# Hash attention and a gated block on one core: parts kept back across a batch's joint, and hash evictions spread among the parts

## The chip, the cores and the metric

One core of a Trainium2 chip. Time is device time in microseconds (us) of one execution; medians of the runs are quoted. TensorE multiplies, VectorE (DVE in the profile) and ScalarE (ACT) work elementwise, and both read the products from PSUM. An **eviction** below reads a hash product out of PSUM and writes its bits: those of k on VectorE, those of q on ScalarE.

## The reference, cut to what matters

```python
# q, k, v: (4, 8, 768, 64); proj: (64, 6)
q_bucket = sum((q @ proj > 0) * powers);  k_bucket likewise        # 6-bit hashes
scores = where(q_bucket == k_bucket, q @ k.T / 8, -1e9)
attn   = softmax(scores) @ v                                       # per batch and head
x      = attn.transpose(0, 2, 1, 3).reshape(3072, 512)
g      = x @ w_gate                                                # 512 -> 1536
out    = (g * sigmoid(g) * (x @ w_val)) @ w_out                    # the gated block
```

## The kernel before

The kernel walks over 16 pairs of heads (four pairs for each of four batches), 12 units of attention to a pair. One **turn** of the main loop does two units: scores, attend, and then parts of the gated block of the *previous* batch, which fill TensorE while the other engines work. The parts stand in the list `atoms` with their sizes; in the seven-product groups below a part is one step, of size 1: two products, which the trace shows as four matmul instructions. A down part (down-projection) has size 2 and shows as six, with 512 columns each.

For batches 1 to 3 the up-projection uses seven products per group (steps 0 to 6) in place of eight. This needs sums of x and of the weights, made on VectorE when the batch's attention ends:

```python
def norm(u):                       # end of half a pair
    ps = score_tile("sum")[:, 0, :] if atoms else bank("sum")
    ...                            # sum product, reciprocal, xT
    if pr == NP - 1 and half == 1:
        push_ffn(b)                # for b > 0: eight sums of x, then sums of weights, then new atoms

def gate(t, g):                    # ScalarE, then VectorE
    nc.scalar.activation(th, g, AF.Tanh, scale=0.5)
    nc.vector.scalar_tensor_tensor(out=t, in0=th, scalar=1.0, in1=g, op0=ALU.add, op1=ALU.mult)
# group steps: 0 copies its product on ScalarE; 1 and 2 one VectorE sum each;
# 3 a gate; 4 two sums and a gate; 5 and 6 a sum and a gate.
# In the value groups a VectorE product takes the place of each gate.
```

For pairs 8 to 15 the four hash products of the next pair share one PSUM tile, taken from the two score buffers:

```python
def hash_blocks():
    ps = front_bank("hps")         # for these pairs: a score buffer
    where = [(name, half) for name in "kq" for half in range(2)]
    for i, (name, half) in enumerate(where):
        nc.tensor.matmul(ps[i * BLOCK : (i + 1) * BLOCK, 0:HQ], ...)
    for i, (name, half) in enumerate(where):
        for to in (0, D):
            sign(name, half, slice(to, to + BLOCK), ps, slice(i * BLOCK, (i + 1) * BLOCK))
            # k: VectorE, q: ScalarE; so k k k k q q q q
```

And the main loop:

```python
for u in range(0, N + 2, 2):       # one turn
    score(u); score(u + 1)
    while due: norm(due.pop(0))
    for x in left: attend(x)
    mine = [up to two steps of the next pair: transposes, hash products]
    ...
    credit += 6.2 if n < 2 * NP else 5.6
    spent = 0
    while atoms and credit >= atoms[0][0]:
        size, atom = atoms.pop(0)
        credit -= size
        spent += size
        atom()
        narrow_on(2 * size)        # conversion of weights, VectorE
        if mine and spent >= 2:
            spent = 0
            mine.pop(0)()
    for step in mine: step()
```

The softmax here doesn't subtract the row's maximum and nothing guards it: scores larger than these inputs give would overflow.

Of the kernel before, what the change touches and what calls it, by code (L numbers as in the profile page):

```python
# [17 lines left out]
def kernel(  # L18
# [13 lines left out]
    B, H, S, D = q.shape  # L32
# [5 lines left out]
    BLOCK = 32  # L38
    NP = H // 2
# [30 lines left out]
    def bank(name):  # L70
        return mm_ps.tile([P, 512], FP32, tag="mm", name=name)
# [40 lines left out]
    def load(n):  # L112
        for name in "qkv":
            fetch(n, name, nc.sync)
# [20 lines left out]
    for _ in range(9):  # L135
        ps = bank("idle")
# [96 lines left out]
    def narrow_on(n):  # L233
        for _ in range(n):
            next(narrowing, None)
# [10 lines left out]
    def front_bank(name):  # L246

        if len(T) > 2 * 2 * NP:
            return score_tile(name)[:, 0, :]
        return bank(name)  # L250

    def front(n):


        def transpose(name, half):
            if (name, n) not in T:
                T[name, n] = opnd.tile([P, S], FP32, tag=name + "T", name=name + "T")
            ps = front_bank("tps")
            for i in range(CH):
                nc.tensor.transpose(ps[:, i * P : (i + 1) * P],  # L260
                                    raws[name, n][:, half * CH + i, :, :].rearrange("p h d -> p (h d)"),
                                    ident)
            nc.scalar.copy(T[name, n][:, half * HQ : (half + 1) * HQ], ps[:, 0:HQ])

        bits["q", n] = sides["q", n % 2]
        bits["k", n] = sides["k", n % 2]

        def sign(name, half, to, ps, at):
            o = bits[name, n][to, half * HQ : (half + 1) * HQ]
            if name == "q":  # L270
                nc.scalar.activation(o, ps[at, 0:HQ], AF.Sign, bias=nudge[to])  # L271
            else:
                nc.vector.tensor_scalar(o, ps[at, 0:HQ], scalar1=above_k[to], scalar2=times_k[to],  # L273
                                        op0=ALU.is_gt, op1=ALU.mult)

        def hash_bits(name, half):
            ps = front_bank("hps")
            nc.tensor.matmul(ps[:, 0:HQ], hash_w[name], T[name, n][:, half * HQ : (half + 1) * HQ],  # L278
                             start=True, stop=True)
            sign(name, half, slice(0, P), ps, slice(0, P))  # L280

        def hash_blocks():

            ps = front_bank("hps")
            where = [(name, half) for name in "kq" for half in range(2)]
            for i, (name, half) in enumerate(where):
                nc.tensor.matmul(ps[i * BLOCK : (i + 1) * BLOCK, 0:HQ], hash_w[name][:, 0:BLOCK],  # L287
                                 T[name, n][:, half * HQ : (half + 1) * HQ], start=True, stop=True)
            for i, (name, half) in enumerate(where):
                for to in (0, D):  # L290
                    sign(name, half, slice(to, to + BLOCK), ps, slice(i * BLOCK, (i + 1) * BLOCK))

        def transpose_blocks(name):
            T[name, n] = opnd.tile([P, S], FP32, tag=name + "T", name=name + "T")
            nc.vector.transpose(T[name, n], raws[name, n].rearrange("p c h d -> p (c h d)"))

        steps = []
        if n > NP:

            for name in "qk":  # L300
                steps.append(lambda name=name: transpose_blocks(name))
        if n >= 2 * NP:
            return steps + [hash_blocks]
        order = [("q", 0), ("k", 0), ("k", 1), ("q", 1)]
        for at in (order[0:2], order[2:3], order[3:4]) if n == 0 else (order,):
            if n <= NP:
                for x in at:
                    steps.append(lambda x=x: transpose(*x))
            for x in at:
                steps.append(lambda x=x: hash_bits(*x))  # L310
        return steps
# [7 lines left out]
    def score(u):  # L319
        n, half, c = units[u]  # L320
        qs = slice(half * HQ, (half + 1) * HQ)
        ks = slice(c * P, (c + 1) * P)
        sc = score_tile("sc")
        for x, start in ((bits, True), (T, False)):
            for h in range(2):
                rows = slice(h * D, (h + 1) * D)
                nc.tensor.matmul(sc[:, h, 0:HQ], x["k", n][rows, ks], x["q", n][rows, qs],  # L327
                                 start=start, stop=not start)
        nc.scalar.activation(ring[u % RING][:, :, 0:HQ], sc[:, :, 0:HQ], AF.Exp, scale=SCALE)  # L329

    def attend(u):
        n, half, c = units[u]
        a = ring[u % RING]
        if c == 0:
            av[n, half] = av_ps.tile([P, 512], FP32, tag="av", name="av")
        ps = av[n, half]
        for h in range(2):
            nc.tensor.matmul(ps[h * D : (h + 1) * D, 0:AW], raws["v", n][:, h, c, :], a[:, h, :],  # L338
                             start=c == 0, stop=c == NCH - 1)
        if c == 1:  # L340
            acc[n, half] = att.tile([P, 2, HQ], FP32, tag="acc", name="acc", bufs=1)
            nc.vector.scalar_tensor_tensor(out=acc[n, half], in0=ring[(u - 1) % RING][:, :, 0:HQ],
                                           scalar=S * EPS / P, in1=a[:, :, 0:HQ],
                                           op0=ALU.add, op1=ALU.add)
        elif c > 1:
            nc.vector.tensor_tensor(acc[n, half], acc[n, half], a[:, :, 0:HQ], op=ALU.add)  # L346
        if c == NCH - 1:
            av[n, half] = att.tile([P, AW], FP32, tag="avs", name="avs", bufs=1)
            nc.scalar.copy(av[n, half], ps[:, 0:AW])

    def norm(u):
        n, half, _ = units[u]
        b, pr = pairs[n]
        if half == 0:
            xT[b, pr] = xp.tile([P, S], FP32, tag="xT", name="xT")
        ps = score_tile("sum")[:, 0, :] if atoms else bank("sum")
        t = acc.pop((n, half))
        for h in range(2):
            nc.tensor.matmul(ps[h * D : (h + 1) * D, 0:HQ], ones, t[:, h, :], start=True, stop=True)  # L359
        a = av.pop((n, half))  # L360
        r = att.tile([P, HQ], FP32, tag="r", name="r", bufs=1)
        nc.vector.reciprocal(r, ps[:, 0:HQ])  # L362
        e = att.tile([P, 1], FP32, tag="e", name="e")
        nc.vector.tensor_scalar(e, a[:, HQ : HQ + 1], scalar1=EPS, scalar2=None, op0=ALU.mult)
        nc.vector.scalar_tensor_tensor(out=xT[b, pr][:, half * HQ : (half + 1) * HQ],
                                       in0=a[:, 0:HQ], scalar=e, in1=r,
                                       op0=ALU.add, op1=ALU.mult)
        if pr == NP - 1 and half == 1:
            push_ffn(b)
# [181 lines left out]
    credit = 0.0  # L551
    left = []
    due = []
    for u in range(0, N + 2, 2):
        n, at = divmod(u, per)
        if u < N:
            if at == (4 if n == 0 else 0) and n + 1 < len(pairs):
                steps.extend(front(n + 1))
            if at == per - 2 and n + 2 < len(pairs):
                load(n + 2)  # L560
            score(u)
            score(u + 1)
        while due:
            norm(due.pop(0))
        for x in left:
            attend(x)
            if units[x][2] == NCH - 1:
                due.append(x)
        left = [u, u + 1]
        mine = [steps.pop(0) for _ in range(2) if (u < 4 or u % per >= 2) and steps]  # L570
        if not atoms:
            credit = 0.0
            for step in mine:
                step()
            narrow_on(3 if u % 12 == 6 else 2)
            continue

        credit += 6.2 if n < 2 * NP else 5.6
        spent = 0
        while atoms and credit >= atoms[0][0]:  # L580
            size, atom = atoms.pop(0)
            credit -= size
            spent += size
            atom()
            narrow_on(2 * size)
            if mine and spent >= 2:
                spent = 0
                mine.pop(0)()
        for step in mine:
            step()  # L590
    while due:
        norm(due.pop(0))
    for _, atom in atoms:
# [33 lines left out]
```

## Time and profile before

| | before |
|---|---|
| time, median of the 3 runs at hand | 1128.71 us |
| TensorE busy, of a span of 1128.2 us | 1093.0 us |
| TensorE idle (span less busy) | 35.2 us |
| of it, waits at three joints between batches | 15.8 us |
| of it, waits that hash evictions cause, three kinds | 6.1 us |

TensorE is the bound, so only its idle time and its clock matter. A matmul at half the granted clock counts as busy, only longer: a loss of clock shows as more "busy", a wait as idle (at a granted clock of 0.50, four matmuls that usually take 1.45 us take 2.90 in the prediction's lines).

### The profile page before, as it was taken

What the parts mean: (1) busy time and instruction counts of PE and PEld (TensorE: products, weight loads), DVE (VectorE), ACT (ScalarE), POOL (GpSimd) and SP (SyncE); (2) the same over time, 40 slices, a digit from 0 to 9 for tenths busy, and PEclk for the clock granted to TensorE, in tenths of its full rate; (3) what the DMA queues carried; (4) which work ended last, traced back from release to release, by engine and by line L of the source; (5) the groups of instructions that cost most, each with busy time, mean ns of one, the idle gap of its engine ahead of it and who ended that gap; (6) DMA issues with size and microseconds to landing.
All of it is one profiled execution on the core that took longest, in us unless ns stands there. A gap on an engine that the chain in (4) does not pass through costs nothing.

```text
span 1128.2 us, 10837 instructions
## 1 busy us (share of the span) xinstructions
PE 1093.0 (97%) x4213; PEld 525.5 (47%) x4213; DVE 700.7 (62%) x1143; ACT 284.8 (25%) x449; POOL 21.1 (2%) x57
## 2 busy tenths in 40 slices
PE   8999999999999989999999997999999997999998
PEld 3444445555544444545544443454544443555543
DVE  4899989999932267777761337667674223667400
ACT  4545222222222213222222222223231120111100
POOL 1000000000000000000000000000000000000000
PEclk9999999999999989999999998999999998999999
DMA  5333422424200220010002021001000000000000
GB/s 141 90 97 64 115 74 89 104 75 117 75 24 19 47 52 1 15 28 1 15 1 61 19 61 29 1 15 29 15 0 10 10 19 19 1 1 0 1 28 28
DMA packets 97843, 44.74 MB, mean 40 GB/s; under 512 B 86016, under 2 KB 90112, under 8 KB 97792
## 3 DMA queue, kind: packets, MB, share of 16 engines
q1 hardware_dynamic: 92032, 26.03, 10.2%
q0 software_dynamic: 4960, 17.83, 5.1%
q8 instruction: 33, 0.54, 0.2%
q10 hardware_dynamic: 800, 0.20, 0.1%
q14 instruction: 18, 0.15, 0.0%
HBM read 37.75 MB, written 6.29 MB: 39 GB/s over the span
## 4 chain that ended last, share of the span: by engine, by line
PE 89%; DVE 6%; ACT 3%; issue 1%; DMA 0%; POOL 0%; SPq 0%; ACTq 0%; DVEq 0%; POOLq 0%
PE up L450 28%; PE po L526 22%; PE sc L327 12%; PE up L396 11%; PE av L338 11%; PE sum L359 2%; ACT A L329 2%; PE hps L278 2%; DVE r L362 1%; DVE kb L273 1%; ACT qb L271 1%; DVE xc L423 1%; DVE acc L346 1%; PE tps L260 1%; PE hps L287 0%
## 5 line engine op out<-in xcount | busy, mean ns | idle before, releaser
L526 PE MATMUL po<-wo,ht 128*128 128x512 f32 x576 | 254.8, 597 | 0.0
L329 ACT ACTIVATE A<-sc 128x768 f32<-128x768 f32 x192 | 154.0, 812 | 213.4 <-PE sc L327 201.2
L362 DVE RECIPROCAL r<-sum 128x384 f32<-128x384 f32 x32 | 81.8, 2556 | 176.0 <-PE sum L359 176.0
L526 PEld LDWEIGHTS po<-wo,ht 128*128 128x128 f32 x576 | 107.3, 190 | 140.2 <-issue 139.1
L327 PE MATMUL sc<-qT,kT 64*128 64x384 f32 x768 | 155.7, 484 | 0.0
L338 PE MATMUL av<-A,vraw 128*64 128x386 f32 x768 | 144.1, 496 | 0.0
L346 DVE TENSOR_TENSOR acc<-acc,A 128x768 f32<-128x768 f32 x128 | 122.2, 954 | 29.8 <-ACT A L329 24.4
L450 PE MATMUL up<-xT,ws 128*128 128x384 f32 x288 | 108.7, 501 | 0.0
L338 PEld LDWEIGHTS av<-A,vraw 128*64 128x64 f32 x768 | 49.3, 136 | 81.4 <-issue 81.2
L327 PEld LDWEIGHTS sc<-qT,kT 64*128 64x128 f32 x768 | 69.2, 190 | 21.0 <-issue 21.0
L450 PEld LDWEIGHTS up<-xT,ws 128*128 128x128 f32 x288 | 55.2, 195 | 44.6 <-issue 7.2
L462 DVE TENSOR_TENSOR ht<-ht,up 128x384 f32<-128x384 f32 x108 | 57.0, 548 | 25.9 <-PE up L450 23.3
L450 PE MATMUL up<-xc,ws 128*128 128x384 f32 x144 | 57.3, 523 | 15.8 <-DVE ws L442 15.8
L462 DVE TENSOR_TENSOR c<-c,up 128x384 f32<-128x384 f32 x108 | 57.6, 549 | 23.7 <-PE up L450 23.0
L396 PE MATMUL up<-xT,wg 128*128 128x384 f32 x192 | 66.9, 491 | 0.4 <-DVE kb L273 0.4
L396 PE MATMUL up<-xT,wv 128*128 128x384 f32 x192 | 66.9, 491 | 0.3 <-DVE wv L226 0.3
L377 ACT ACTIVATE c<-up 128x384 f32<-128x384 f32 x42 | 20.6, 491 | 184.0 <-PE up L396 100.9
L327 PE MATMUL sc<-qb,kb 64*128 64x384 bf16 x384 | 63.9, 329 | 1.7 <-ACT qb L271 0.9
L450 PE MATMUL up<-xT,wv 128*128 128x384 f32 x144 | 54.3, 501 | 2.9 <-ACT ht L483 2.9
L450 PE MATMUL up<-xc,wg 128*128 128x384 f32 x144 | 53.9, 498 | 2.3 <-DVE c L378 2.3
L530 ACT COPY o<-po 128x512 f32<-128x512 f32 x24 | 14.1, 587 | 159.1 <-PE po L526 158.8
L450 PE MATMUL up<-xc,wv 128*128 128x384 f32 x144 | 53.2, 492 | 0.0
(99 smaller groups left out, 934.8 us busy)
## 6 DMA issues: line engine op xcount, KB each, us to landing
vraw<-in_v_dram SPq DMA_DIRECT2D x16, 384.0 KB, 3.3
words<-in_moe_w_val_dram POOLq DMA_DIRECT2D x12, 512.0 KB, 3.8
words<-in_moe_w_out_dram POOLq DMA_DIRECT2D x12, 512.0 KB, 3.6
out_dram<-o SPq DMA_DIRECT2D x24, 256.0 KB, 2.0
words<-in_moe_w_gate_dram POOLq DMA_DIRECT2D x10, 512.0 KB, 3.9
qraw<-in_q_dram SPq DMA_DIRECT2D x48, 96.0 KB, 3.4
kraw<-in_k_dram SPq DMA_DIRECT2D x46, 96.0 KB, 3.3
qraw<-in_q_dram SPq DMA_DIRECT2D x8, 192.0 KB, 3.6
```

The source lines that it names most:

```text
L278: nc.tensor.matmul(ps[:, 0:HQ], hash_w[name], T[name, n][:, half * HQ : (half + 1) * HQ], start=True, stop=True)
L327: nc.tensor.matmul(sc[:, h, 0:HQ], x["k", n][rows, ks], x["q", n][rows, qs], start=start, stop=not start)
L329: nc.scalar.activation(ring[u % RING][:, :, 0:HQ], sc[:, :, 0:HQ], AF.Exp, scale=SCALE)
L338: nc.tensor.matmul(ps[h * D : (h + 1) * D, 0:AW], raws["v", n][:, h, c, :], a[:, h, :], start=c == 0, stop=c == NCH - 1)
L346: nc.vector.tensor_tensor(acc[n, half], acc[n, half], a[:, :, 0:HQ], op=ALU.add)
L359: nc.tensor.matmul(ps[h * D : (h + 1) * D, 0:HQ], ones, t[:, h, :], start=True, stop=True)
L362: nc.vector.reciprocal(r, ps[:, 0:HQ])
L377: nc.scalar.activation(th, g, AF.Tanh, scale=0.5)
L396: nc.tensor.matmul(ps, w[:, j, f * P : (f + 1) * P], x[j][:, halves[half]], start=j == 0, stop=j == NJ - 1)
L450: nc.tensor.matmul(ps, a[:, j], xs[j], start=start and j == 0, stop=j == 1, skip_group_check=True)
L462: nc.vector.tensor_tensor(out_, a, b, op=op)
L526: nc.tensor.matmul(ps, hs[f, half][:, i * P : (i + 1) * P], wo[:, f, :], start=f == 0, stop=f == NF - 1)
```

## The change

The intent is twofold. Smaller credits leave some down parts of a batch in the list when the next batch's sums are being made, so that TensorE has work there. And the evictions of a late hash product no longer come in one block: a step may now return further steps, and the evictions become four steps of one k and one q each, which take turns with the parts. The pace of the steps changes as well: one step per size, where it was one per two sizes.

```diff
-            for i, (name, half) in enumerate(where):
-                for to in (0, D):
-                    sign(name, half, slice(to, to + BLOCK), ps, slice(i * BLOCK, (i + 1) * BLOCK))
+            def evict(half, to):
+                for i, x in enumerate(where):
+                    if x[1] == half:
+                        sign(x[0], half, slice(to, to + BLOCK), ps,
+                             slice(i * BLOCK, (i + 1) * BLOCK))
+
+            return [lambda half=half, to=to: evict(half, to) for half in range(2) for to in (0, D)]
 ... (the loop; the branch without atoms alike)
-        credit += 6.2 if n < 2 * NP else 5.6
-        spent = 0
+        credit += 5.75 if n < 2 * NP else 5.5
         while atoms and credit >= atoms[0][0]:
             size, atom = atoms.pop(0)
             credit -= size
-            spent += size
             atom()
             narrow_on(2 * size)
-            if mine and spent >= 2:
-                spent = 0
-                mine.pop(0)()
-        for step in mine:
-            step()
+            while mine and size:
+                size -= 1
+                mine[:1] = mine[0]() or []
+        while mine:
+            mine[:1] = mine[0]() or []
```

More of the change, by code (lines that the diff above doesn't have):

```diff
@@ L582 @@
             credit -= size
-            spent += size
             atom()
             narrow_on(2 * size)
-            if mine and spent >= 2:
-                spent = 0
-                mine.pop(0)()
-        for step in mine:
-            step()
+            while mine and size:
+                size -= 1
+                mine[:1] = mine[0]() or []
+        while mine:
+            mine[:1] = mine[0]() or []
     while due:
```

## The prediction

> **What bounds the kernel now.** I read the page first (busy shares, the slices), then who waited for whom on TensorE, then the timeline around the longest waits, then the granted clock in stretches just behind them. From the page:
>
> ```profile
> PE 1093.0 (97%) x4213; PEld 525.5 (47%) x4213; DVE 700.7 (62%) x1143; ACT 284.8 (25%) x449; POOL 21.1 (2%) x57
> ...
> PE   8999999999999989999999997999999997999998
> ...
> PEclk9999999999999989999999998999999998999999
> ```
>
> TensorE is busy 97% of 1128.2 us, so the time is TensorE's work plus its 35 us of idleness. The slices show where: start and end, and dips near 400, 700 and 950 us, each with a lower granted clock. TensorE's waits, longest first (us in total, times, longest):
>
> ```profile
> PE up L450 <- DVE ws L442: 15.8, 3, 6.0
> PE up L450 <- ACT ht L483: 2.9, 1, 2.9
> PE up L450 <- DVE c L378: 2.3, 1, 2.3
> PE sum L359 <- ACT A L329: 2.2, 8, 1.0
> ...
> PE sc L327 <- ACT qb L271: 0.9, 2, 0.6
> ```
>
> Three waits of 15.8 us together stand where a batch's attention is over, its sums are made on VectorE and the list of gated-block parts is empty. One of them in the timeline (start us, us, instruction):
>
> ```profile
> 400.80 2.56 DVE L362 RECIPROCAL r<-sum 128x384 f32<-128x384 f32 x1 [15.77 <-PE sum L359]
> ...
> 406.76 1.02 DVE L423 TENSOR_TENSOR xc<-xc,xT 128x384 f32<-128x384 f32 x2
> ...
> 408.15 0.42 DVE L442 TENSOR_TENSOR ws<-wg 128x256 f32<-128x256 f32 x1
> ...
> 408.72 2.90 PE L450 MATMUL up<-xc,ws 128*128 128x384 f32 x4 [5.19 <-DVE ws L442]
> ```
>
> The chain reciprocal, xT, eight sums (L423), weight sums takes 8 us; TensorE has 2.8 us to do meanwhile, then stands 5.19 us. Its four matmuls then take 2.90 us instead of the usual 1.45. The clock just behind the wait (busy us by engine, PEclk):
>
> ```profile
> 408.70:414.00 5.30, 5.28 (x9) 2.88 (x10) 4.41 (x9) 0.00 (x0) 0.00 (x0) 0.50 0.01 3
> ```
>
> So the wait costs another 5.3 x 0.50 = 2.65 us. The second kind of wait is a late hash product:
>
> ```profile
> 496.55 2.72 DVE L273 TENSOR_SCALAR kb<-hps,columns 32x384 bf16<-32x384 f32 x4 [0.26 <-PE hps L287]
> ...
> 499.36 2.33 ACT L271 ACTIVATE qb<-hps,columns 32x384 bf16<-32x384 f32 x4 [7.03 <-DVE kb L273]
> 501.72 0.49 ACT L377 ACTIVATE c<-up 128x384 f32<-128x384 f32 x1
> ...
> 502.86 2.69 PE L450 MATMUL up<-xc,wg 128*128 128x384 f32 x4 [2.31 <-DVE c L378]
> ```
>
> Four VectorE evictions, then four ScalarE ones, hold up the tanh of a gate by 5 us; its bank is needed, and TensorE stands 2.31 us.
>
> **What the Trainium skill says.** "TensorE: Matmul & The Clock Gate", Part 1, "What's actually happening": half clock after an idle window of about 3.4 us, full again after about 3.4 us of sustained work. The trace agrees on the half (0.50 for 5.3 us), but shows loss already behind a wait of 2.31 us. The specification table at that page's head calls the queues of ScalarE and VectorE strict FIFO; the tanh at 501.72 behind four evictions agrees. "PSUM — Partial Sum Buffer", "PSUM bank collisions raise a hardware error": two engines may not access one bank and quadrant at once, different quadrants may. Here k and q lie in different quadrants, yet ScalarE starts (499.36) only when VectorE is done (499.27): the program orders them by tile.
>
> **The change part by part.** No instruction is added or removed; the order changes.
>
> (1) Credit. A size is four matmul instructions, 1.29 us. A batch has 24 turns of two units. Before: 24 x 6.2 = 149 against 144 sizes, then 24 x 5.6 = 134 against 132, so the list is empty at each joint. After: 24 x 5.75 = 138, of which 136 can be spent, leaves 8; then 8 + 132 - 24 x 5.5 = 8 again. At each joint 8 sizes (four down parts, 2.64 us each) stand behind the sum product. Three run in the same turn: 7.9 us, plus 1.45 of attend and the next turn's 3.2 and 2.6, against a chain of 8 to 9 us. All three waits should go, at the last joint too (10.5 us of parts). Gain: 15.8 us, and clock behind them: 5.3 x 0.50 + 5.0 x 0.45 + 4.8 x 0.41 = 6.9. Sum 22.7. The sum now takes a score buffer and waits for an exponential, 0.2 us each, some 0.7 in all.
>
> (2) Evictions. Each step is now one k on VectorE (0.67 us) and then one q on ScalarE (0.58), four such pairs after successive parts. The old waits go: 2.94 + 2.31 + 0.9 us, and clock behind the two longer ones (502.86 to 507.70 and 704.45 to 709.30 against 3.0 to 3.1 us at full clock): 1.8 + 1.7. Gain 9.7.
>
> But the hash bank is one of two score buffers, and the second score of the next turn needs it. Its release is now the last q, behind the sums and gates of four parts on an in-order VectorE, and in the changed program's order each k waits for the q before it. The worst turn, pair 10 (gate steps 4, hash, 5, 6, 0, 1), t = 0 at the hash product, durations from the rows (sum 0.55, tanh 0.52 with 0.1 ahead, gate product 0.56, weight sum 0.42, hops 0.09):
> - step 4: sums 0.25-1.27, gate to 2.47; step 5: sum to 3.02, gate to 4.22; k1 4.22-4.89, q1 to 5.55;
> - step 6: sum to 5.44, tanh behind q1 to 6.07, gate to 6.66; k2 to 7.33, q2 to 7.99;
> - four weight sums to 9.0; k3 to 9.67, q3 to 10.33; sum of step 1 to 10.2; k4 10.4-11.1, q4 to 11.7.
>
> TensorE is through with its four parts at 0.78 + 1.39 + 3 x 1.29 = 6.0 and with the first score at 6.9. New wait: 11.8 - 6.9 = 4.9 us. The same working gives for pairs 8 to 15: 0.8, 0.5, 4.9, 3.1, 2.2, 0.1, 4.5, 3.1, together 19.2 us. (Pair 12 has only two down parts: four round trips of 1.4 us against 3.5 us of work.) Clock behind the four long ones some 2.2 each, behind pair 12's perhaps 1: 9.8. Loss 29.
>
> (3) The early pairs' steps move a little closer. From 118 to 310 us VectorE is busy 176.7 of 192 us; 0 to 1 us more.
>
> **Sum:** 1128.7 - 22.7 - 9.7 + 0.7 + 29 = 1126. Part 1 is near certain, the 29 is an estimate from eight chains worked by hand, in which every delay of VectorE falls on the bank. I shade it down by a few us, to 1121.
>
> **Rivals.** (a) The hash waits don't appear, or last under 1 us, because TensorE's own small delays let VectorE catch up: then 1128.7 - 22.7 - 9.7 + 2 = 1098. For it speaks that the present order shows only 0.9 us of such score waits; against it, that now k's and q's follow the product at once, 5.3 us after it, and no longer. (b) The new score waits eat the gain: 1120 to 1128; for it speaks the working above. (c) The joints stay, because the chain gets longer behind other VectorE work: against it, VectorE idled 15.77 us before the reciprocal, and down parts give it nothing. It would add 10 or so. (d) VectorE becomes the bound while weights are converted: the conversion is tied to the parts, and fewer parts per turn make it thinner; a few us at most.
>
> **Range and chances.** (b) is the likeliest, with errors of 6 us or so on the 29; (a) has about one chance in seven. That gives 1121 us, 8 times in 10 between 1103 and 1131. Faster by over 2% means under 1106: 0.15. Slower by over 2% would need the long waits and the joints as well: 0.02. Within 2%: 0.83.
>
> **What would show it.** Step 1: the waits for ws gone from TensorE's list and PEclk near 1.0 at the three joints. Step 2: the waits for th/c and ht behind evictions gone, and in their place score products waiting for qb, four of them of 3 to 5 us, with clock lost behind them. If those are absent, the prediction is wrong by 20 us and more; if ws waits stay, by up to 20 the other way.

## The result, and the profile after

The changed kernel takes **1124.99 us** (median of 4 runs, 1123.71 to 1126.00) against 1128.76 for the kernel before in the runs at its side. Ratios here are the mean time of one kernel's runs over that of the other's of the same rounds, so not quite the ratio of the medians: 0.9961, interval 0.9944 to 0.9979. That is 0.4% faster, and within 2%.

The page of the changed kernel, the same three lines as before (PE and PEclk: 40 slices of the span, TensorE's busy share and granted clock in tenths):

```profile
PE 1091.4 (97%) x4213; PEld 523.0 (47%) x4213; DVE 702.1 (62%) x1143; ACT 284.3 (25%) x449; POOL 21.0 (2%) x57
...
PE   8999999999999999989899999999989999999998
...
PEclk9999999999999999989999999998999999999999
```

The dips at 400, 675 and 950 us are gone; the ones left stand in other slices. Span less busy gives 1123.5 - 1091.4 = 32.1 us idle, against 35.2. What TensorE waits for, longest first (us in total, times, longest):

```profile
PE sc L332 <- ACT qb L271: 16.6, 6, 4.3
PE sum L364 <- ACT A L334: 2.5, 10, 0.6
...
PE up L455 <- DVE c L467: 1.0, 2, 0.5
```

(Lines from 292 on are renumbered, most of them by 5: L455 here is L450 of before, L332 is L327.) The waits for weight sums (15.8 us) and the two kinds of up product behind hash evictions (5.2) are gone. In their place scores wait for the q evictions: 16.6 us instead of 0.9.

The joint at 400 us, now at 392 (timeline: start us, us, engine and instruction):

```profile
392.41 2.56 DVE L367 RECIPROCAL r<-sum 128x384 f32<-128x384 f32 x1 [18.47 <-PE sum L364]
393.59 7.99 PE L531 MATMUL po<-wo,ht 128*128 128x512 f32 x18
...
399.76 0.42 DVE L447 TENSOR_TENSOR ws<-wg 128x256 f32<-128x256 f32 x1
...
408.23 1.56 PE L455 MATMUL up<-xT,wg 128*128 128x384 f32 x4
```

Three down parts run during the chain of sums. The weight sums are ready at 401 us; TensorE comes for the first up product only at 408, and waits for nothing. The longest new wait is the turn of pair 10, whose hash product precedes these lines:

```profile
479.39 0.34 PE L332 MATMUL sc<-qb,kb 64*128 64x384 bf16 x2
...
482.76 0.55 DVE L467 TENSOR_TENSOR ht<-ht,up 128x384 f32<-128x384 f32 x1
482.77 0.58 ACT L271 ACTIVATE qb<-hps,columns 32x384 bf16<-32x384 f32 x1 [1.34 <-DVE kb L273]
483.38 0.67 DVE L273 TENSOR_SCALAR kb<-hps,columns 32x384 bf16<-32x384 f32 x1
...
484.08 0.57 ACT L271 ACTIVATE qb<-hps,columns 32x384 bf16<-32x384 f32 x1 [0.74 <-DVE kb L273]
...
484.70 0.50 PE L332 MATMUL sc<-qb,kb 64*128 64x384 bf16 x2 [4.33 <-ACT qb L271]
```

The first score starts at 479.39. The second needs the buffer that the hash product holds, and the last q leaves it at 484.65. TensorE stands 4.33 us, and behind it the granted clock is 0.50 for the 4.5 us from 484.7 to 489.2, which costs 2.2 us more.

### The profile page after: what moved, and what is told of

Read it like the earlier page. It is cut to its first block, busy times and chain, and to the rows that moved or that the text cites. A ratio compares the mean times of both kernels' runs of the same rounds, so it can differ in the third digit from the quotient of the medians.

```text
span 1123.5 us, 10819 instructions
## 1 busy us (share of the span) xinstructions
PE 1091.4 (97%) x4213; PEld 523.0 (47%) x4213; DVE 702.1 (62%) x1143; ACT 284.3 (25%) x449; POOL 21.0 (2%) x57
## 4 chain that ended last, share of the span: by engine, by line
PE 85%; DVE 9%; ACT 3%; issue 1%; DMA 0%; POOL 0%; SPq 0%; DVEq 0%; ACTq 0%; POOLq 0%
PE up L455 27%; PE po L531 22%; PE sc L332 11%; PE av L343 11%; PE up L401 9%; PE sum L364 2%; ACT A L334 2%; PE hps L278 1%; DVE kb L273 1%; DVE r L367 1%; DVE acc L351 1%; ACT qb L271 1%; DVE c L383 1%; PE tps L260 1%; PE hps L287 1%
## 5 line engine op out<-in xcount | busy, mean ns | idle before, releaser
L332 PE MATMUL sc<-qT,kT 64*128 64x384 f32 x768 | 156.6, 486 | 0.0
L343 PE MATMUL av<-A,vraw 128*64 128x386 f32 x768 | 149.0, 510 | 0.0
L455 PE MATMUL up<-xT,ws 128*128 128x384 f32 x288 | 106.1, 491 | 0.0
L332 PE MATMUL sc<-qb,kb 64*128 64x384 bf16 x384 | 64.0, 330 | 17.4 <-ACT qb L271 16.6
L332 PEld LDWEIGHTS sc<-qT,kT 64*128 64x128 f32 x768 | 69.3, 190 | 19.6 <-issue 19.6
L455 PEld LDWEIGHTS up<-xT,ws 128*128 128x128 f32 x288 | 53.9, 191 | 43.3 <-issue 4.8
L401 PE MATMUL up<-xT,wv 128*128 128x384 f32 x192 | 67.3, 492 | 0.5 <-DVE wv L226 0.3
L401 PE MATMUL up<-xT,wg 128*128 128x384 f32 x192 | 66.9, 491 | 0.5 <-DVE ht L386 0.5
L332 PEld LDWEIGHTS <-kb 64*128 64x128 bf16 x384 | 19.3, 93 | 88.1 <-issue 73.7
L273 DVE TENSOR_SCALAR kb<-hps,columns 32x384 bf16<-32x384 f32 (+1 forms) x48 | 32.1, 669 | 35.2 <-PE hps L287 22.6
L455 PE MATMUL up<-xT,wg 128*128 128x384 f32 x144 | 54.0, 498 | 0.0
L455 PE MATMUL up<-xc,ws 128*128 128x384 f32 x144 | 52.9, 490 | 1.0 <-DVE c L467 1.0
```

The costliest lines, as they stand in the source:

```text
L273: nc.vector.tensor_scalar(o, ps[at, 0:HQ], scalar1=above_k[to], scalar2=times_k[to], op0=ALU.is_gt, op1=ALU.mult)
L332: nc.tensor.matmul(sc[:, h, 0:HQ], x["k", n][rows, ks], x["q", n][rows, qs], start=start, stop=not start)
L343: nc.tensor.matmul(ps[h * D : (h + 1) * D, 0:AW], raws["v", n][:, h, c, :], a[:, h, :], start=c == 0, stop=c == NCH - 1)
L401: nc.tensor.matmul(ps, w[:, j, f * P : (f + 1) * P], x[j][:, halves[half]], start=j == 0, stop=j == NJ - 1)
L455: nc.tensor.matmul(ps, a[:, j], xs[j], start=start and j == 0, stop=j == 1, skip_group_check=True)
```

## The experiments

**Theory.** The new score waits come from the spreading: each k eviction stands in VectorE's in-order queue behind the sums and gates of one more part, and the q behind it, so the score buffer is held until the last of them. **Rival A:** the new credits moved the hash products into worse turns, and the order of evictions doesn't matter. **Rival B:** the hand-overs between the two engines (each k waits for the q before it, each q for its k: seven in a chain) make it long. Eight kernels ran, each with 5 rounds, all with right results; the first four share one chip's runs of the kernel before (median 1129.74 us), the last four another's (1129.72). At the 2% mark only one of them is clearly faster (the k's at once, one turn later); the intervals of four others lie across 0.98.

### Credits alone

```diff
 (the kernel before)
-        credit += 6.2 if n < 2 * NP else 5.6
+        credit += 5.75 if n < 2 * NP else 5.5
```

> Part one alone: the kernel before with the credits 5.75 and 5.5, evictions all at once as before. Theory (the spreading makes the score waits): the three ws waits (15.8 us) are gone and stay gone; TensorE's waits of scores for qb fall from 16.6 us to under 4 us; some waits of up products behind the bulk of evictions remain, 2 to 6 us; time 1106 to 1113 us. Rival A (the new credits move the hash products to turns where VectorE is behind, so they would make the score waits with either order of evictions): score waits stay above 12 us and the time is 1120 us or more.

Measured: **1106.55 us**, ratio 0.9803 (0.979 to 0.9816). TensorE's waits:

```profile
PE sc L327 <- ACT qb L271: 5.1, 5, 1.6
PE up L450 <- ACT c L483: 3.4, 2, 1.7
PE sum L359 <- ACT A L329: 2.5, 10, 0.6
```

The three joints are filled, and the score waits are 5.1 us, a little above the 4 that were expected but far from 16.6. Busy time falls to 1082.9 us, 10.1 less than before: the granted clock is 1.0, and none of these waits, 1.7 us at most, lowered it. Rival A is out as the main cause. The old waits for c L378 and ht L483 are gone as well, though the evictions are in one block as before. So the shift of the hash products against the steps removed them, and not the spreading. But others of their kind came instead: twice step 0's copy (L483) stands behind the q's, and the hash waits are 8.5 us in all (5.1 + 3.4) against 6.1 before. What is gained on them is the clock, which is full behind all of these.

### Spreading alone

```diff
 (the changed kernel)
-        credit += 5.75 if n < 2 * NP else 5.5
+        credit += 6.2 if n < 2 * NP else 5.6
```

> Part two alone: the changed kernel with the old credits 6.2 and 5.6. Theory: the three ws waits of about 15 us are back, and the score waits for qb are there as well, 12 to 20 us in six or so; time 1138 to 1150 us, that is slower than both. Rival A: without the new credits the spreading helps as intended, score waits under 4 us, time 1119 to 1125 us.

Measured: **1144.72 us**, ratio 1.0135 (1.0121 to 1.0149), slower than both.

```profile
PE up L455 <- DVE ws L447: 15.9, 3, 6.0
PE sc L332 <- ACT qb L271: 15.1, 7, 3.6
```

Joints and score waits stand side by side. The two parts nearly add up as ratios: 0.9803 x 1.0135 = 0.9935, against 0.9961 together. The change is a gain of some 23 us with a loss of some 18 on top of it (1124.99 - 1106.55).

### All evictions at once, the rest of the change kept

```diff
-            def evict(half, to): ...
-            return [lambda half=half, to=to: evict(half, to) for half in range(2) for to in (0, D)]
+            for i, (name, half) in enumerate(where):
+                for to in (0, D):
+                    sign(name, half, slice(to, to + BLOCK), ps, slice(i * BLOCK, (i + 1) * BLOCK))
```

> The changed kernel, credits and pace of the steps kept, but the eight evictions follow the hash product at once (four of VectorE, then four of ScalarE) instead of one pair per part. Theory: chain from hash product to last q is 0.2 + 2.7 + 2.4 us = 5.3 behind its end, so with four parts behind it (6.9 us to the second score) the score waits go, except in the turn with two down parts (about 2 us); where the turn has steps 0 to 3 the copy of P1 is held behind the q's and costs some 2 us, twice. Time 1103 to 1110 us. Rival A: score waits stay above 12 us.

Measured: **1106.86 us**, ratio 0.9802 (0.9788 to 0.9815).

```profile
PE up L451 <- ACT c L484: 3.4, 2, 1.7
PE sum L360 <- ACT A L330: 2.5, 10, 0.6
PE sc L328 <- ACT qb L271: 1.6, 1, 1.6
```

As expected in the time and in both waits: the score waits fall from 16.6 to 1.6 us (the turn with two down parts), and twice a product waits 1.7 us for step 0's copy, which stands behind the q's on ScalarE. (Four small waits for VectorE's sums, 1.4 us in all, come beside them.) The order of evictions alone makes 18 us, with credits and pace held. Whether the pace is old (credits alone) or new (here) matters nothing to the sum.

### Two k, two k, two q, two q

```diff
-            def evict(half, to): ...
-            return [lambda half=half, to=to: evict(half, to) for half in range(2) for to in (0, D)]
+            def evict(name, half):
+                i = where.index((name, half))
+                for to in (0, D):
+                    sign(name, half, slice(to, to + BLOCK), ps, slice(i * BLOCK, (i + 1) * BLOCK))
+
+            return [lambda x=x: evict(*x) for x in where]
```

> The changed kernel with as many steps, spread the same way, but two of VectorE, two of VectorE, two of ScalarE, two of ScalarE, so there is one hand-over between the engines instead of seven. Theory (VectorE's in-order queue: each step stands behind sums and gates of one more part): the longest score waits stay, 4.1 us for pair 10 and 2.6 for pair 11, sum 12 to 17 us, time within 3 us of the changed kernel's 1125. Rival B (the hand-overs between ScalarE and VectorE, 7 of 0.66 us each, make the chain long): each of the long waits falls by 2 to 3 us, sum under 7 us, time 1110 to 1116.

Measured: **1121.48 us**, ratio 0.9929 (0.9916 to 0.9941). Score waits 15.0 us in 7; pair 10's is 3.86 instead of 4.33, pair 11's 2.43 instead of 3.15. Six of seven hand-overs are gone and 1.6 us of 16.6 with them. That alone doesn't size rival B, since the edit moves work both ways. In pair 10 the last k ends 2.4 us behind the start of the first score instead of 4.7, but four q's (2.33 us) follow it instead of one. The changed kernel's own trace is more direct:

```profile
478.06 0.57 ACT L271 ACTIVATE qb<-hps,columns 32x384 bf16<-32x384 f32 x1 [1.26 <-DVE kb L273]
...
479.08 0.56 DVE L383 SCALAR_TENSOR_TENSOR c<-th,c 128x384 f32<-128x384 f32 x1 [0.65 <-ACT th L382]
...
479.65 0.67 DVE L273 TENSOR_SCALAR kb<-hps,columns 32x384 bf16<-32x384 f32 x1
...
621.23 0.57 ACT L271 ACTIVATE qb<-hps,columns 32x384 bf16<-32x384 f32 x1 [0.74 <-DVE kb L273]
621.84 0.67 DVE L273 TENSOR_SCALAR kb<-hps,columns 32x384 bf16<-32x384 f32 x1 [0.64 <-ACT qb L271]
```

In pair 10 the second k starts as the gate ahead of it ends (479.64), a full us after the first q is done (478.63). In pair 12, among down parts, each k does wait for the q before it. VectorE sits idle for a q before a k six times in the whole run, 5.2 us in all, three times each in pairs 8 and 12, whose score waits are 0.45 and 1.64 us. The other 14.5 us come in pairs where VectorE never idles for a q. Even pair 12 would hardly gain: with all eight at once it waits 1.58. So rival B is out as the cause of the long waits. The time fell by 3.5 us against the changed kernel's 1124.99, half a microsecond more than the theory allowed: busy time is lower by 1.6 us too (1089.8 against 1091.4), and the clock is full now behind pair 11's wait (it was 0.63), though not behind pair 15's, which is just as long (2.43 us, clock 0.67).

### The k's at once, the q's after the next part

```diff
-            def evict(half, to): ...
-            return [lambda half=half, to=to: evict(half, to) for half in range(2) for to in (0, D)]
+            def evict(of):
+                for i, (name, half) in enumerate(where):
+                    if name == of:
+                        for to in (0, D):
+                            sign(name, half, slice(to, to + BLOCK), ps,
+                                 slice(i * BLOCK, (i + 1) * BLOCK))
+
+            evict("k")
+            return [lambda: evict("q")]
```

> The changed kernel, the four k evictions right behind the hash product, the four q's after the next part. Theory: the chain is 2.7 us of k's, then the next part's copy or tanh, then 2.4 us of q's. Where steps 0 to 3 follow, the copy of P1 now runs ahead of the q's (3.4 us of waits less than with all at once); behind gate step 4 the q's stand behind a tanh and end at 8.6 us against 6.9: score waits of 1.7 us, twice; the turn with two down parts 1.6 as with all at once. Sum of hash waits about 5 us, no loss of clock, time 1104 to 1107, within 2 us of all at once. Rival A2 (any spreading at all costs as much as the full one): score waits over 10 us, 1115 or more.

Measured: **1107.86 us**, ratio 0.9809 (0.9797 to 0.9822): slightly above what was expected, and by another way. The copy of step 0 still waits behind the q's (1.7 us, twice), because a down part has size 2 and so takes two steps: in that turn hash product, k's and q's came together after all. Pair 10's score waited 0.5 us, not 1.7. A small amount of spreading does no harm, but it bought nothing here either.

### The same, one turn later

```diff
 (the kernel of the last experiment)
-            return steps + [hash_blocks]
+            return steps + [lambda: None] * 2 + [hash_blocks]
```

> As the k's at once, and the hash product one turn later, where six parts (or three down parts) stand in the turn instead of five (or two). Theory: the second score is wanted at 8.2 us behind the hash product instead of 6.9, the q's end at 8.7 at the latest: hash waits under 2 us in all. From the 1106.9 us with all at once, which still waited 6.4 us, this gives 1100 to 1103 us. Rival: if the product's turn doesn't matter, 1104 to 1107 as without the shift.

Measured: **1103.23 us** (1102.96 to 1103.76), ratio **0.9769** (0.9756 to 0.9781): the fastest kernel, 2.3% below the kernel before. No score waits for a q any more; the longest waits that are left:

```profile
PE sum L366 <- ACT A L336: 4.2, 10, 1.5
PE up L457 <- DVE c L469: 1.4, 4, 0.5
```

The expectation was 1100 to 1103 us. What it left out is that the sum product comes in the turn behind and now waits for an exponential that runs late, 1.5 us in two of the turns.

### Spreading, one turn later

```diff
 (the changed kernel)
-            return steps + [hash_blocks]
+            return steps + [lambda: None] * 2 + [hash_blocks]
```

> The changed kernel's one-by-one spreading, hash product one turn later, so with one part more of room. Theory (what counts is which sums and gates stand between the evictions): pair 10 and 14 now have four gate steps between, the last q at 13.9 us against 8.2: waits of about 5.7; pair 9 and 13 3.5; pair 11 and 15 1.5; sum 15 to 22 us in spite of the room, time 1125 to 1135, no better than the changed kernel. Rival C (the number of parts left in the turn is what counts, each part of room gives 1.3 us): waits fall from 16.6 to about 9 us, time 1112 to 1117.

Measured: **1121.37 us** (1116.50 to 1122.64), ratio 0.9918 (0.99 to 0.9937); score waits 14.3 us in 8. This fits neither number. The theory's 5.7 us for pair 10 was wrong by an oversight: behind the product stand steps of a value group there, which have no tanh, and the wait was 1.87. Pair 9 now waits 3.05 us (2.59 in pair 13, its like), where it waited less than 0.3 in the changed kernel: there the product followed a down part, whose two steps took the first k and q at once, and steps 0 to 3 came behind; here gate steps stand between the evictions. The sum fell by 2.3 us only. By turns, the two traces separate what stands between the evictions from the room, that is, TensorE's time from the hash product to the first score:

| steps between the evictions | changed kernel, room 6.14 us | one turn later, room 7.43 us |
|---|---|---|
| 5 and 6 with gates, then 0 and 1 | 4.33 (pair 10), 3.88 (14) | 3.05 (pair 9), 2.59 (13) |
| 3 to 6 of a value group | 3.15 (pair 11), 3.15 (15) | 1.87 (pair 10), 1.86 (14) |

```profile
556.44 0.34 PE L332 MATMUL sc<-qb,kb 64*128 64x384 bf16 x2 [3.15 <-ACT qb L271]
...
428.59 0.34 PE L332 MATMUL sc<-qb,kb 64*128 64x384 bf16 x2 [3.05 <-ACT qb L271]
...
497.74 0.34 PE L332 MATMUL sc<-qb,kb 64*128 64x384 bf16 x2 [1.87 <-ACT qb L271]
```

(The first line is the changed kernel's, the others this one's.) With the same steps between, one part more of room takes 1.28 or 1.29 us off the wait in all four, just a part's time, as rival C had it. With the same room, the gate and weight-sum steps cost 0.7 to 1.2 us more than the value steps, as the theory had it (pair 14 has three weight sums where pair 10 has four). The sum hardly fell because the later turn put the costly steps behind pairs 9 and 13, which had waited for nothing.

### All at once, one turn later

```diff
 (the kernel with all evictions at once)
-            return steps + [hash_blocks]
+            return steps + [lambda: None] * 2 + [hash_blocks]
```

> All eight evictions at once behind the hash product, one turn later. Theory: no score waits; behind gate step 4 (pairs 9 and 13) the tanh of step 5 stands behind the q's, so a bank comes free 1.5 us late, twice; hash waits about 3 us, time 1101 to 1105, that is 2 to 5 us below all at once in the earlier turn.

Measured: **1107.09 us**, ratio 0.9804 (0.9792 to 0.9817), a miss: no gain over the earlier turn. There are no score waits, and the bank wait behind pairs 9 and 13 came as said, but it was 1.9 us each, the clock was lowered behind the first of them in the profiled run, and the sum products wait 4.5 us in all instead of 2.5. With the k's first and the q's behind one tanh, those 1.9 us don't arise; that, with the clock, is most of the 4 us to the best kernel.

## Why the prediction was right, and where it wasn't

- **The joints** behaved as said. Credits alone gave 23.2 us by the medians (1129.74 - 1106.55). The prediction's terms for joints, old waits and sums make 22.7 + 9.7 - 0.7 = 31.7, and 8.5 us of hash waits were left (5.1 + 3.4): 23.2. That it fits to the tenth is luck; the terms don't include the smaller waits. The extra waits of sums were put at 0.7 us and are 0.3 (2.5 against 2.2).
- **The old hash waits** went, but the prediction booked their 9.7 us under the spreading. The run with credits alone shows that they go without it, with 8.5 us of other hash waits in their place at full clock. The attribution was wrong.
- **The new hash waits** were said to be 19.2 us in eight pairs and are 16.6 in six:

| pair | 8 | 9 | 10 | 11 | 12 | 13 | 14 | 15 |
|---|---|---|---|---|---|---|---|---|
| predicted, us | 0.8 | 0.5 | 4.9 | 3.1 | 2.2 | 0.1 | 4.5 | 3.1 |
| measured, us | 0.45 | under 0.3 | 4.33 | 3.15 | 1.64 | under 0.3 | 3.88 | 3.15 |

- **The clock** behind them was put at 9.8 us. With credits alone the clock is full (busy 1082.9), in the changed kernel it is not (1091.4): 8.5 us. By pair, from the granted clock in the 5 to 7 us behind each wait (0.69, 0.63, 0.66, 0.68), some 2.3 (pair 10), 1.7 (11), 2.5 (14) and 1.7 (15), and none behind pair 12. So the 29 us of loss were 25.
- **The total** owes something to luck. The working gave 1126 us and the kernel took 1125.0, but with 25 in place of 29 its terms give 1122. Of the missing 3 us, 1.7 net are small waits that its sum left out (for c and ht, up to 0.5 us each, and for a transfer of k), and the profiled execution of the kernel before, from which its waits were read, was 1.3 us above the median.
- **The shading** was the weak step: "I shade it down by a few us, to 1121" had no measurement behind it. The loss was indeed put 4 us too high, and still the shaded total lay farther from what was measured. Rival (a), one chance in seven, didn't happen; the queue arithmetic that stood above it spoke against it.
- **Rivals** (c) and (d) didn't happen: no wait for ws at the joints, and the waits for converted weights are 0.3 us as before.
- That each k waits for the q before it was named as part of the cause. It held VectorE up only in pairs 8 and 12, where 2.1 of the 16.6 us fell.

What stays open: why the clock falls behind some waits and not behind others just as long (last section). A hash tile in one of the three up banks, which would free the score buffers, could not be run: the simulation ahead of the chip finds a deadlock, with the evictions spread and with all at once alike. So the place of the last eviction is not the whole reason; it was not looked into.

## What to carry to other kernels

A buffer is held until its last reader is done, and on an in-order engine that reader waits for everything issued ahead of it (pair 10's last q left the score buffer 4.3 us after TensorE wanted it): spreading evictions out smooths the engine, but if the buffer is scarce the wait moves to its next user. Before spreading, work through one turn by hand from the trace's durations, the last eviction against the next claim; here that gave 4.9 us where 4.33 were measured. And test the parts of a change apart: a total of 0.4% was a gain of 2.0% with a loss laid over it.

## What the Trainium skill lacked or had wrong

- "TensorE: Matmul & The Clock Gate", Part 1, gives an idle window of about 3.4 us for the return to half clock; its passage on frequent micro-idles gives no length. Shorter waits lowered it here, and not always: 2.31 us did in the kernel before. Two waits of 2.43 us with pairs of the same engine left it at 1.00 (pair 11) and 0.67 (pair 15). In the kernel "spreading, one turn later" 1.87 us did and 2.59 us did not, as the granted clock just behind them shows:

```profile
497.70:500.20 2.50, 2.46 (x10) 0.90 (x11) 1.05 (x3) 2.00 (x3) 0.00 (x0) 0.57 0.00 0
703.50:706.50 3.00, 2.93 (x18) 1.14 (x17) 1.10 (x1) 1.64 (x3) 0.00 (x0) 1.00 0.00 0
```

  (Columns as in the prediction's line of the clock; the last but two is PEclk.) The page's free-running window would make the phase decide. No run here sets the phase, so this is left open; it may also be behind that kernel's spread of 6 us between runs, whose mean granted clock goes from 0.992 to 0.998.
- "PSUM — Partial Sum Buffer", "PSUM bank collisions raise a hardware error", lets two engines read different quadrants of one bank at once, but doesn't say that a program whose instructions wait for each other over one tile gives this up. Here k's and q's lie in different quadrants and still run one after the other: with all at once, q's start at 478.83 us, when the k's of 476.02 us (2.71 us) are done, and the trace names them as what ScalarE waited for.
- No page has what a buffer's hold costs when its evictions stand among other work of an in-order engine: 16.6 us of waits and 8.5 us of clock here.
